# One norm product a head, weight signs on ScalarE, wider value rows and early fills in an attention and expert kernel on one core

## The chip, the cores and the metric

The kernel runs on one core of a Trainium2 chip. The core has TensorE (PE: matrix products; PEld is its loading of the stationary operand), VectorE (DVE), ScalarE (ACT), GpSimd (POOL) and SyncE (SP), which here only starts the transfers. Each engine works through its own list of instructions in order and waits at semaphores. The metric is the time of one execution in microseconds on the device; less is better.

## What is computed

Four batches of 768 tokens with eight heads of 64 go through an attention with a window of 16 to each side and 24 pooled keys and values (a maximum over 32 keys, a mean over 32 values), and the result through a gated layer with 512 features and 1,024 inner ones:

```python
k_sum = k.reshape(B, H, nb, block, D).max(axis=3)
v_sum = v.reshape(B, H, nb, block, D).mean(axis=3)
scores_s = scale * np.einsum('bhsd,bhnd->bhsn', q, k_sum) + np.log(block)
scores_all = np.concatenate([np.where(mask_l, scores_l, -1e9), scores_s], axis=-1)
a = np.exp(scores_all - scores_all.max(-1, keepdims=True))
x = np.matmul(a / (a.sum(-1, keepdims=True) + 1e-09), np.concatenate([v, v_sum], axis=2))
...
xk = mu_k * x + (1.0 - mu_k) * x_prev
xr = mu_r * x + (1.0 - mu_r) * x_prev
k = np.maximum(xk @ w_k, 0.0)
out = 1.0 / (1.0 + np.exp(-(xr @ w_r))) * (k * k @ w_v)
```

The weights are sent as 64-bit floats, in pairs of 32-bit words, and are turned into 32-bit floats on the chip.

## The kernel before

The work is cut into eight stages, one for each half (384 tokens) of each batch. In every stage there are four attention units, one for each pair of heads. A unit (`unit`) computes the scores of 64-query windows against 120 keys each (L466, twelve products of two passes each), adds the mask and takes the maximum on VectorE (L477), the exponential with its sum on ScalarE (L481), the inverse of the sums on VectorE (L487, L488), multiplies by it on GpSimd (`norm`, L493: three instructions of 120 columns for each of the two heads), transposes on TensorE (L500), copies the transposed weights out (L504) and multiplies by v (L513). Then the stage mixes neighbouring tokens (`mix`, L535 to L549), computes the gate (L567 to L569; in the first stage L580, in full float32) with its sigmoid (L558), and runs eight expert steps: a product with a column block of w_k (`first`, L601), ReLU and square (L608, L610), and a product with a row block of w_v (`second`, L627). The first stage works in float32 with unsplit weights. From the second on each weight and each activation is split into two parts (`split`, L349 to L352) and three products replace one.

Weights come in through `weight`: a load into one of three `st` buffers (L310), a product of the high words with 2^-112 on ScalarE or GpSimd (L318, L321), a shift of the low words into the single buffer `we` (L325), the sign taken from the high words and put into `we` (L328), and a join of both into the weight (L332), the last three on VectorE. `load_set` brings in k and v of a pair (L367, L371); v has 120 rows: 48 keys to each side of 24 rows for the pooled values, which are spread into it (L431, L440). GpSimd's list also holds a reload instruction, shown as ISA, which the framework puts ahead of the first instruction that needs it.

Nothing is issued in the order of the source. `Plan` takes every operation with its reads and writes, its due time and its length from the table `LENGTH`, and `schedule` lays them out engine by engine: of the operations that are ready it takes the one that can start first, then the one due first. The order that comes out is fixed and is what each engine's list holds. A transfer is counted with `DMA_NS_PER_BYTE`, and operations named in `LOCKS` are held apart from GpSimd's. Fills (`warm`, L680) are products of the identity with itself whose result nobody reads; they take a buffer of the `mm` pool and are dropped when the first gate product is placed:

```python
if o.name == "gate32" and spare:
    for w in spare:
        ...
    ready["PE"] = [x for x in ready["PE"] if x[0].name != "warm"]
```

Of the kernel before, what the change touches and what calls it, by code (L numbers as in the profile page):

```python
# [20 lines left out]
P = 128  # L21
# [21 lines left out]
    result=695, wbits=340, wor=612, wsub=612, tiny=60,  # L43
    exp=380, pts=380, vm=160, mixa=520, cast=405, relu=525, square=530, sigmoid=500, wscale=570, wcast=530,
    norm=345, wscale_p=640, wcast_p=640, mixa_p=860, kcopy_p=630, evac_a=375, fill=735,
)
TAIL = dict(PE=0, DVE=85, ACT=95, POOL=0, SP=0)
LATENCY = dict(PE=260, DVE=110, ACT=110, POOL=150, SP=0)
DMA_NS_PER_BYTE = 1 / 290.0
DMA_FIXED = 2000  # L50
# [6 lines left out]
SLACK = 400  # L57
WARM = 150
COLD = 10000
EARLY = 15000  # L60
# [38 lines left out]
class Plan:  # L99
# [36 lines left out]
    def schedule(self):  # L136
# [24 lines left out]
        for o in self.ops:  # L161
            if not waiting[o]:
                released(o)
        spare = [o for o in self.ops if o.name == "warm"]
        while any(ready.values()):
            best = None
            for e, now in engines.items():
                pick = None
                for o, at in ready[e]:
                    start, need, ok = max(at, now, o.due - EARLY if e == "SP" else 0), {}, True  # L170
# [49 lines left out]
            order.append(o)  # L220
            if o.name == "gate32" and spare:

                for w in spare:
                    for x in w.bufs:
                        x.left -= 1
                        if not x.left:
                            free_slots[x.pool].append((start, x.place))
                spare = []
                ready["PE"] = [x for x in ready["PE"] if x[0].name != "warm"]
            if o.name == "warm":  # L230
                spare.remove(o)
            for s in o.succ:
# [7 lines left out]
def tile_kernel(ctx: ExitStack, tc: tile.TileContext, q, k, vT, v, mask, ident, pool, sel, mu, w_k, w_v, w_r, out):  # L240
# [60 lines left out]
    def weight(name, i, src, last, due=None):  # L301
        st, we, wc = buf("st"), buf("we"), buf("wc")
        wf = w_f[name, i] = buf("wc") if last else buf("w", F32, False)
        shape = src.shape
        whole = [(wc, 0)]

        def load():
            s = src.bitcast(U32)
            d = st.t.rearrange("p (c a) -> p c a", c=shape[1]) if len(shape) == 3 else st.t
            nc.sync.dma_start(out=d, in_=s)  # L310

        def words():
            w = st.t.rearrange("p (a b) -> p a b", b=2)
            return w[:, :, 1], w[:, :, 0]


        def scale_act():
            nc.scalar.activation(wc.t.bitcast(F32), words()[0].bitcast(F32), AF.Copy, scale=2.0**-112)  # L318

        def scale_pool():  # L320
            nc.gpsimd.tensor_scalar(  # L321
                out=wc.t.bitcast(F32), in0=words()[0].bitcast(F32), scalar1=2.0**-112, scalar2=1.0, op0=ALU.mult, op1=ALU.mult)

        def low():
            nc.vector.tensor_scalar(out=we.t, in0=words()[1], scalar1=29, scalar2=None, op0=ALU.logical_shift_right)  # L325

        def sign():
            nc.vector.scalar_tensor_tensor(  # L328
                out=we.t, in0=words()[0], scalar=0x80000000, in1=we.t, op0=ALU.bitwise_and, op1=ALU.bitwise_or)

        def join():
            nc.vector.scalar_tensor_tensor(  # L332
                out=wf.t.bitcast(U32), in0=wc.t, scalar=3, in1=we.t, op0=ALU.logical_shift_left, op1=ALU.bitwise_or)

        op("SP", "load", due, load, writes=[(st, 0)], size=P * 4096)
        op("ACT", "wscale", None, scale_act, reads=[(st, 0)], writes=whole, other=("POOL", "wscale_p", scale_pool))
        op("DVE", "wbits", None, low, reads=[(st, 0)], writes=[(we, 0)])
        op("DVE", "wor", None, sign, reads=[(st, 0), (we, 0)], writes=[(we, 0)])
        op("DVE", "wor", None, join, reads=[(we, 0), *whole], writes=[(wf, 0)])

# [20 lines left out]
    def load_set(b, p):  # L361
# [83 lines left out]
    def unit(b, p, hf, e, due):  # L445
# [45 lines left out]
        for h in range(2):  # L491
            for i in range(NSL):
                op("POOL", "norm", None, lambda h=h, i=i: nc.gpsimd.tensor_scalar(  # L493
                    out=y[h].t[:, i, :], in0=y[h].t[:, i, :], scalar1=rc.t[:, NSL * h + i:NSL * h + i + 1],
                    scalar2=1.0, op0=ALU.mult, op1=ALU.mult),
                   reads=[(y[h], i), (rc, 0)], writes=[(y[h], i)])

# [77 lines left out]
    def gate_parts(x, z):  # L575

        ps = [buf("mm") for _ in range(NTT)]
        for p in range(NPAIR):
            for t in range(NTT):
                op("PE", "gate32", GATE0 - (NPAIR - 1 - p) * FIRST + 930 * t, lambda p=p, t=t: nc.tensor.matmul(  # L580
                    ps[t].t, x[p].t[:, t * P:(t + 1) * P], w_f["wr", p].t, start=(p == 0), stop=(p == NPAIR - 1)),
                   reads=[(x[p], 0), (w_f["wr", p], 0), *([(ps[t], 0)] if p else [])], writes=[(ps[t], 0)])
# [89 lines left out]
    for i in range(NCK):  # L672
        weight("wr", i, w_r[i * P:(i + 1) * P, :], False)
# [4 lines left out]
    spare = buf("mm", F32, False)  # L678
    for _ in range(WARM):
        op("PE", "warm", 1.0e8, lambda: nc.tensor.matmul(  # L680
            spare.t[:, 0:P], ident_sb, ident_sb, start=True, stop=True), reads=IDENT, writes=[(spare, 0)])
    sets, gates = [], []
# [120 lines left out]
```

## Time and profile before

| | us |
|---|---|
| median of 3 runs (lowest, highest) | 474.1 (472.27, 476.43) |
| the profiled execution | 475.29 |
| its span, first to last instruction | 473.5 |

The granted TensorE clock is 0.993 on the mean. The page's picture of the span in 40 slices of 11.8 us shows each engine's busy share and the clock in tenths:

```profile
PE   2798799989899999999999999999999999999996
DVE  3599789989453566527554565529354554222223
ACT  3578987878785756418886756428886655231311
POOL 0453470734133201302442201304242201000000
PEclk9999889999999999999999999999999999999999
DMA  7995368986110209807200219707100010001001
```

The first ten slices hold the loading of all weights, the first stage and most of the preparation of the second; from then on the stages repeat. Rows of a timeline give start, length, engine, line, operation, output and inputs, shape and count, and in brackets the idle time before and what ended it. Rows of groups give the busy time, the mean of one instruction in ns, and the idle time before.

### The profile page before, as it was taken

What the parts mean: (1) busy time and instruction counts of PE and PEld (TensorE: products, weight loads), DVE (VectorE), ACT (ScalarE), POOL (GpSimd) and SP (SyncE); (2) the same over time, 40 slices, a digit from 0 to 9 for tenths busy, and PEclk for the clock granted to TensorE, in tenths of its full rate; (3) what the DMA queues carried; (4) which work ended last, traced back from release to release, by engine and by line L of the source; (5) the groups of instructions that cost most, each with busy time, mean ns of one, the idle gap of its engine ahead of it and who ended that gap; (6) DMA issues with size and microseconds to landing.
All of it is one profiled execution on the core that took longest, in us unless ns stands there. A gap on an engine that the chain in (4) does not pass through costs nothing.

```text
span 473.5 us, 9475 instructions
## 1 busy us (share of the span) xinstructions
PE 447.6 (95%) x3438; PEld 357.9 (76%) x3438; DVE 267.0 (56%) x865; ACT 292.6 (62%) x815; POOL 112.5 (24%) x236
## 2 busy tenths in 40 slices
PE   2798799989899999999999999999999999999996
PEld 2664455546688888997778888997778889888995
DVE  3599789989453566527554565529354554222223
ACT  3578987878785756418886756428886655231311
POOL 0453470734133201302442201304242201000000
PEclk9999889999999999999999999999999999999999
DMA  7995368986110209807200219707100010001001
GB/s 245 257 261 158 105 207 262 289 263 148 51 59 12 68 1 304 211 0 228 60 8 9 78 37 301 212 1 219 35 9 9 12 43 26 1 0 68 0 1 66
DMA packets 27013, 51.16 MB, mean 108 GB/s; under 512 B 2903, under 2 KB 14807, under 8 KB 26967
## 3 DMA queue, kind: packets, MB, share of 16 engines
q1 hardware_dynamic: 26967, 50.56, 36.7%
q8 instruction: 27, 0.44, 0.4%
q14 instruction: 19, 0.16, 0.1%
HBM read 42.49 MB, written 6.29 MB: 103 GB/s over the span
## 4 chain that ended last, share of the span: by engine, by line
PE 67%; ACT 12%; DVE 8%; DMA 8%; issue 2%; POOL 1%; SPq 1%; ACTq 0%; POOLq 0%; DVEq 0%
PE mm L627 23%; PE mm L601 22%; ACT y L481 5%; PE pt L500 4%; PE av L513 4%; DMA kt<-in_k 3%; PE mm L567 3%; PE mm L569 3%; PE mm L568 3%; PE sc L466 2%; DMA pool_sb<-in_pool 2%; PE mm L580 2%; ACT L481 2%; DMA st<-in_w_k 1%; POOL y L493 1%
## 5 line engine op out<-in xcount | busy, mean ns | idle before, releaser
L601 PE MATMUL mm<-xs,w 128*128 128x384 f32 x736 | 152.1, 355 | 0.6 <-DVE w L332 0.6
L601 PEld LDWEIGHTS mm<-xs,w 128*128 128x128 f32 x736 | 131.3, 190 | 13.9 <-issue 3.7
L493 POOL TENSOR_SCALAR y<-y,rc 128x120 f32<-128x120 f32 x192 | 93.9, 507 | 156.1 <-DVE rc L488 131.6
L627 PE MATMUL mm<-w,kh 128*128 128x512 f32 x336 | 91.9, 402 | 0.0
L608 ACT ACTIVATE r<-mm 128x384 f32<-128x384 f32 x64 | 31.2, 488 | 93.9 <-PE mm L601 93.8
L481 ACT ACTIVATE y<-y,mn 128x120 f32<-128x120 f32 x192 | 73.5, 386 | 10.7 <-DVE mn L477 10.4
L627 PEld LDWEIGHTS mm<-w,kh 128*128 128x128 f32 x336 | 60.7, 188 | 11.1 <-DVE kl L616 0.2
L614 DVE CAST kh<-r 128x384 fp32r<-128x384 f32 x44 | 15.9, 362 | 74.9 <-ACT r L610 74.8
L477 DVE CUSTOM_DVE_ANT_0 y<-sc,mask_sb 128x120 f32<-128x120 f32 x192 | 42.5, 277 | 22.9 <-PE sc L466 19.6
L627 PE MATMUL mm<-w,kl 128*128 128x512 f32 x168 | 52.4, 407 | 0.1
L549 DVE TENSOR_TENSOR xs<-xa,xs 128x384 fp32r<-128x384 f32 x56 | 30.4, 558 | 23.6 <-ACT xs L547 23.2
L500 PE MATMUL pt<-ident_sb,y 128*120 128x128 f32 x192 | 33.9, 285 | 6.4 <-POOL y L493 6.0
L504 ACT COPY pts<-pt 120x384 f32<-120x384 f32 x64 | 30.3, 473 | 15.6 <-PE pt L500 15.4
L466 PE MATMUL sc<-kt,qt 64*64 64x120 f32 x768 | 30.4, 289 | 8.6 <-DMA pool_sb<-in_pool 6.8
L500 PEld LDWEIGHTS pt<-ident_sb,y 128*120 128x120 f32 x192 | 22.8, 139 | 19.0 <-POOL y L493 9.6
L481 ACT ACTIVATION_READ_ACCUMULATOR y<-y,mn 128x1 f32 x192 | 36.3, 189 | 0.0
L541 DVE SCALAR_TENSOR_TENSOR xa<-vx,mu_sb,xa 128x384 f32<-128x384 f32 x56 | 33.8, 630 | 2.7 <-ACT xa L535 1.8
L627 PEld LDWEIGHTS mm<-w,kl 128*128 128x128 f32 x168 | 30.0, 188 | 6.5 <-DVE kl L616 0.5
L466 PEld LDWEIGHTS sc<-kt,qt 64*64 64x64 f32 x768 | 22.2, 143 | 16.7 <-DVE kt L393 6.8
L567 PE MATMUL mm<-w,xs 128*128 128x512 f32 x84 | 33.6, 400 | 1.1 <-ACT r L608 0.8
L610 ACT ACTIVATE r<-r 128x384 f32<-128x384 f32 x64 | 33.6, 525 | 1.2
L616 DVE TENSOR_TENSOR kl<-r,kh 128x384 fp32r<-128x384 f32 x56 | 31.7, 566 | 4.3 <-ACT kh L615 1.3
(64 smaller groups left out, 548.1 us busy)
## 6 DMA issues: line engine op xcount, KB each, us to landing
vx<-in_v SPq DMA_DIRECT2D x32, 360.0 KB
kt<-in_k SPq DMA_DIRECT2D x15, 544.0 KB
qt<-in_q SPq DMA_DIRECT2D x32, 192.0 KB
out<-z SPq DMA_DIRECT2D x24, 256.0 KB
st<-in_vT SPq DMA_DIRECT2D x12, 384.0 KB
st<-in_w_k SPq DMA_DIRECT2D x8, 512.0 KB
st<-in_w_v SPq DMA_DIRECT2D x8, 512.0 KB
st<-in_w_r SPq DMA_DIRECT2D x4, 512.0 KB
```

Of the source, the lines that this page charges most:

```text
L466: nc.tensor.matmul(sc[h].t[cs, i, 0:NK], qt.t[hs, n * QW:(n + 1) * QW], kt.t[hs, w * KB:w * KB + NK], start=True, stop=True,)
L477: op("DVE", "mask", None, lambda h=h, i=i, var=var: nc.vector.tensor_tensor_reduce(out=y[h].t[:, i, :], in0=sc[h].t[:, i, 0:NK], in1=mask_ ...
L481: op("ACT", "exp", None, lambda h=h, i=i: nc.scalar.activation(y[h].t[:, i, :], y[h].t[:, i, :], AF.Exp, bias=mn[h].t[:, i:i + 1], scale=-1.0,
L493: op("POOL", "norm", None, lambda h=h, i=i: nc.gpsimd.tensor_scalar(out=y[h].t[:, i, :], in0=y[h].t[:, i, :], scalar1=rc.t[:, NSL * h + i: ...
L500: nc.tensor.transpose(out=pt[h].t[0:NK, i * P:(i + 1) * P], in_=y[h].t[:, i, :], identity=ident_sb)
L541: op("DVE", "mixd", None, lambda: nc.vector.scalar_tensor_tensor(out=xa.t, in0=xt.t[:, 1 + lo:1 + lo + HT], scalar=mu_sb[:, which, p:p + 1 ...
L567: nc.tensor.matmul(ps.t, xh.t[:, ts], h, start=(p == 0), stop=False)
L601: nc.tensor.matmul(ps.t[:, 0:HT], w.t[:, p * P:(p + 1) * P], (x[p] if single else x[p][s]).t, start=(n == 0), stop=(n == len(terms) * NPAI ...
L608: op("ACT", "relu", None, lambda: nc.scalar.activation(r.t, ps.t[:, 0:HT], AF.Relu), reads=[(ps, 0)], writes=[(r, 0)])
L610: op("ACT", "square", None, lambda: nc.scalar.activation(r.t, r.t, AF.Square), reads=[(r, 0)], writes=[(r, 0)])
L616: op("DVE", "sub", None, lambda: nc.vector.tensor_tensor(out=kl.t, in0=r.t, in1=kh.t.bitcast(F32), op=ALU.subtract), reads=[(r, 0), (kh, 0 ...
L627: nc.tensor.matmul(acc[t].t, a.t[:, t * P:(t + 1) * P], v.bitcast(F32) if single else v, start=start, stop=stop)
```

## The change

There are six parts.

1. **Norms.** The three `norm` instructions of a head become one product of the whole 128 x 360 block with the inverse sums, each repeated over 120 columns. The table's `norm` goes from 345 to 750.
2. **Signs.** The scale of the high words becomes a parametric ReLU on ScalarE with slope -2^32 for negative words, which puts the sign where the join's shift moves it to the top. The sign instruction on VectorE goes, and so does GpSimd as the other engine for the scale.
3. **Values.** v is sent with 128 rows (eight of zeros) in place of 120 and its load writes the whole tile.
4. **Weights.** The blocks of w_k, w_v and w_r are laid out on the host, so that every load is 128 contiguous rows of 4,096 bytes; w_k's were four pieces of 1,024.
5. **Fills.** They multiply a tile of zeros, which GpSimd sets at the start, so that they need no transfer, and write an unused part of the `pt` bank. Up to 260 may be placed; the planner puts one on TensorE wherever nothing else could start within 300 ns, until 110 us of its own count.
6. **First gate.** Its three sigmoids are one operation behind all three gate products. The table's cost of a byte goes from 1/290 to 1/330 ns.

```diff
-            for i in range(NSL):
-                op("POOL", "norm", None, lambda h=h, i=i: nc.gpsimd.tensor_scalar(
-                    out=y[h].t[:, i, :], in0=y[h].t[:, i, :], scalar1=rc.t[:, NSL * h + i:NSL * h + i + 1],
-                    scalar2=1.0, op0=ALU.mult, op1=ALU.mult),
-                   reads=[(y[h], i), (rc, 0)], writes=[(y[h], i)])
+            op("POOL", "norm", None, lambda h=h: nc.gpsimd.tensor_tensor(
+                out=y[h].t, in0=y[h].t, in1=rc.t[:, NSL * h:NSL * h + NSL].unsqueeze(2).broadcast_to([P, NSL, NK]), op=ALU.mult),
+               reads=[(rc, 0)] + [(y[h], i) for i in range(NSL)], writes=[(y[h], i) for i in range(NSL)])
...
-            nc.scalar.activation(wc.t.bitcast(F32), words()[0].bitcast(F32), AF.Copy, scale=2.0**-112)
+            wc.t.bitcast(F32), words(1).bitcast(F32), AF.Prelu, scale=2.0**-112, alpha=-2.0**32),
...
-        def sign():
-            nc.vector.scalar_tensor_tensor(
-                out=we.t, in0=words()[0], scalar=0x80000000, in1=we.t, op0=ALU.bitwise_and, op1=ALU.bitwise_or)
...
-                out=windows(vw[hf]), in_=v[b, p, hf]),
-               writes=[(vw[hf], "a"), (vw[hf], "b")], size=NK * HW * 512)
+                out=vw[hf].t[:, 0:S], in_=v[b, p, hf]),
+               writes=[(vw[hf], "a"), (vw[hf], "b")], size=P * HW * 512)
...
-        weight("wk", j, w_k[:, j * P:(j + 1) * P].rearrange("(c p) n -> p c n", p=P), False)
-        weight("wv", j, w_v[j * P:(j + 1) * P, :], j == NCV - 1)
+        weight("wk", j, w_k[j], False)
+        weight("wv", j, w_v[j], j == NCV - 1)
...
+                if fill and (pick is None or pick[2] > fill[0] + GAP):
+                    pick = None, fill[1], fill[0]
...
+    op("POOL", "tiny", -1.0e6, lambda: nc.gpsimd.memset(zero_sb, 0.0), writes=ZERO)
+    spare = pools["pt"][0][:, 512 - P:512]
     for _ in range(WARM):
-        op("PE", "warm", 1.0e8, lambda: nc.tensor.matmul(
-            spare.t[:, 0:P], ident_sb, ident_sb, start=True, stop=True), reads=IDENT, writes=[(spare, 0)])
+        op("PE", "warm", 1.0e8, lambda: nc.tensor.matmul(spare, zero_sb, zero_sb, start=True, stop=True), reads=ZERO)
...
-        for t in range(NTT):
-            sigmoid(ps[t], z[t])
+        def sigmoids():
+            for t in range(NTT):
+                nc.scalar.activation(z[t].t, ps[t].t, AF.Sigmoid)
+
+        op("ACT", "sigmoid3", None, sigmoids, reads=[(a, 0) for a in ps], writes=[(a, 0) for a in z])
```

The planner lays everything out anew, so the change moves instructions on every engine. Line numbers are those of each kernel. ScalarE around the first gate, before: `z` is the sigmoid's output, `y` a head's scores, `wc` a scaled weight, `r` an expert block.

```order
L558 ACT_TABLE_LOAD
L558 ACTIVATE z_108<-mm_135 128x512
L481 ACT_TABLE_LOAD
L481 ACTIVATE y_91,sm_100<-y_91,mn_95 128x120 x3
L481 ACTIVATE y_92,sm_100<-y_92,mn_96 128x120 x3
L558 ACT_TABLE_LOAD
L558 ACTIVATE z_109<-mm_133 128x512
L558 ACTIVATE z_110<-mm_134 128x512
L318 ACTIVATE wc_127<-st_123 128x512
L608 ACTIVATE r_116<-mm_132 128x384
L610 ACTIVATE r_116<-r_116 128x384
L481 ACT_TABLE_LOAD
```

The same place on ScalarE in the changed kernel:

```order
L456 ACTIVATE y_91,sm_100<-y_91,mn_95 128x120 x3
L456 ACTIVATE y_92,sm_100<-y_92,mn_96 128x120 x3
L559 ACT_TABLE_LOAD
L559 ACTIVATE z_108<-mm_133 128x512
L559 ACTIVATE z_109<-mm_135 128x512
L559 ACTIVATE z_110<-mm_132 128x512
L585 ACTIVATE r_116<-mm_134 128x384
L477 COPY pts_107<-pt_130 120x384
L587 ACTIVATE r_116<-r_116 128x384
L307 ACTIVATE wc_127<-st_123 128x512
L307 ACTIVATE wc_126<-st_124 128x512
L456 ACT_TABLE_LOAD
```

The six exponentials of the unit moved ahead of the sigmoids, and two of the four table loads are gone. Over the whole list there are 20 table loads against 22, and none stands at the parametric ReLU (L307).

VectorE ahead of the last gate product, before (`we`, `wc`, `w`: the weight's parts; `xs`: mixed tokens; `vx`: v):

```order
L325 TENSOR_SCALAR we_125<-st_122 128x512
L352 TENSOR_TENSOR w_0_516<-w_0_495,w_0_500 128x512
L328 SCALAR_TENSOR_TENSOR we_125<-st_122,we_125 128x512
L332 SCALAR_TENSOR_TENSOR w_0_524<-wc_127,we_125 128x512
L325 TENSOR_SCALAR we_125<-st_123 128x512
L328 SCALAR_TENSOR_TENSOR we_125<-st_123,we_125 128x512
L352 TENSOR_TENSOR w_0_559<-w_0_524,w_0_529 128x512
L332 SCALAR_TENSOR_TENSOR w_0_563<-wc_126,we_125 128x512
L541 SCALAR_TENSOR_TENSOR xs_0_561<-vx_79,mu_sb,xs_0_561 128x384
```

And in the changed kernel:

```order
L327 TENSOR_TENSOR w_0_516<-w_0_496,w_0_505 128x512
L514 SCALAR_TENSOR_TENSOR xs_0_513<-vx_76,mu_sb,xs_0_513 128x384
L406 COPY vx_77<-vm_88 24x768
L310 TENSOR_SCALAR we_125<-st_123 128x512
L327 TENSOR_TENSOR w_0_533<-w_0_510,w_0_525 128x512
L312 SCALAR_TENSOR_TENSOR w_0_547<-wc_126,we_125 128x512
L327 TENSOR_TENSOR w_0_555<-w_0_547,w_0_549 128x512
L514 SCALAR_TENSOR_TENSOR xs_0_557<-vx_79,mu_sb,xs_0_557 128x384
```

The sign instructions (L328) are gone from between the shift and the join; one split more stands ahead of the mix of the last pair.

GpSimd's list at the start, before:

```order
L522 MEMSET vx_79 128x1
L493 ISA
L493 TENSOR_SCALAR y_91<-y_91,rc_102 128x120 x3
L493 TENSOR_SCALAR y_92<-y_92,rc_102 128x120 x3
L493 TENSOR_SCALAR y_93<-y_93,rc_103 128x120 x3
L493 TENSOR_SCALAR y_94<-y_94,rc_103 128x120 x3
L431 COPY vx_69<-vm_85 24x768
L321 TENSOR_SCALAR wc_126<-st_122 128x512
```

And in the changed kernel:

```order
L495 MEMSET vx_79 128x1
L368 COPY kt_62<-ks_83 128x12x24
L467 ISA
L467 TENSOR_TENSOR y_91<-y_91,rc_102 128x360
L467 TENSOR_TENSOR y_92<-y_92,rc_102 128x360
L467 TENSOR_TENSOR y_93<-y_93,rc_103 128x360
L406 COPY vx_68<-vm_85 24x768
L467 TENSOR_TENSOR y_94<-y_94,rc_103 128x360
```

The reload (ISA) moved behind a copy of the pooled keys into `kt`, which VectorE made before, and the copy waits for the second pair's keys. TensorE's list begins with 13 fills, has 11 between the first two sets of scores, 7 ahead of the first pooled values, eight more before the gates, and five on either side of the first transposes behind the gates: 49 fills against 15.

More of the change, by code (lines that the diff above doesn't have):

```diff
@@ L43 @@
     result=695, wbits=340, wor=612, wsub=612, tiny=60,
-    exp=380, pts=380, vm=160, mixa=520, cast=405, relu=525, square=530, sigmoid=500, wscale=570, wcast=530,
-    norm=345, wscale_p=640, wcast_p=640, mixa_p=860, kcopy_p=630, evac_a=375, fill=735,
+    exp=380, pts=380, vm=160, mixa=520, cast=405, relu=525, square=530, sigmoid=500, sigmoid3=4000, wscale=570, wcast=530,
+    norm=750, wscale_p=640, wcast_p=640, mixa_p=860, kcopy_p=630, evac_a=375, fill=735,
 )
@@ L48 @@
 LATENCY = dict(PE=260, DVE=110, ACT=110, POOL=150, SP=0)
-DMA_NS_PER_BYTE = 1 / 290.0
+DMA_NS_PER_BYTE = 1 / 330.0
 DMA_FIXED = 2000
@@ L57 @@
 SLACK = 400
-WARM = 150
-COLD = 10000
+WARM = 260
+WARM_END = 110000
+GAP = 300
+COLD = 5000
 EARLY = 15000
@@ L163, in schedule @@
                 released(o)
-        spare = [o for o in self.ops if o.name == "warm"]
         while any(ready.values()):
@@ L167, in schedule @@
             for e, now in engines.items():
-                pick = None
+                pick = fill = None
+                if e == "PE" and now > WARM_END:
+                    ready[e] = [x for x in ready[e] if x[0].name != "warm"]
                 for o, at in ready[e]:
+                    if o.name == "warm":
+                        fill = max(now, at), o
+                        continue
                     start, need, ok = max(at, now, o.due - EARLY if e == "SP" else 0), {}, True
@@ L220, in schedule @@
             order.append(o)
[L221 to L231, printed above, removed]
             for s in o.succ:
@@ L276, in tile_kernel @@
     sel_sb = const.tile([P, NS], F32, name="sel_sb")
-    MASK, IDENT, MU, OM, POOLM, SEL = [((x, 0),) for x in ("mask", "ident", "mu", "om", "pool", "sel")]
+    zero_sb = const.tile([P, P], F32, name="zero_sb")
+    MASK, IDENT, MU, OM, POOLM, SEL, ZERO = [((x, 0),) for x in ("mask", "ident", "mu", "om", "pool", "sel", "zero")]
     op("SP", "load", None, lambda: nc.sync.dma_start(out=mask_sb, in_=mask), writes=MASK, size=P * 3 * NK * 4)
@@ L303, in weight @@
         wf = w_f[name, i] = buf("wc") if last else buf("w", F32, False)
[L304 to L325, printed above, removed]
-        def sign():
-            nc.vector.scalar_tensor_tensor(
-                out=we.t, in0=words()[0], scalar=0x80000000, in1=we.t, op0=ALU.bitwise_and, op1=ALU.bitwise_or)
@@ L331, in join @@
[L331 to L338, printed above, removed]
@@ L339, in weight, with words @@
-        op("DVE", "wor", None, join, reads=[(we, 0), *whole], writes=[(wf, 0)])
+        def words(n):
+            return st.t.rearrange("p (a b) -> p a b", b=2)[:, :, n]
+        op("SP", "load", due, lambda: nc.sync.dma_start(out=st.t, in_=src.bitcast(U32)), writes=[(st, 0)], size=P * 4096)
+        op("ACT", "wscale", None, lambda: nc.scalar.activation(
+            wc.t.bitcast(F32), words(1).bitcast(F32), AF.Prelu, scale=2.0**-112, alpha=-2.0**32),
+           reads=[(st, 0)], writes=[(wc, 0)])
@@ L341, in split @@
+        op("DVE", "wbits", None, lambda: nc.vector.tensor_scalar(
+            out=we.t, in0=words(0), scalar1=29, scalar2=None, op0=ALU.logical_shift_right), reads=[(st, 0)], writes=[(we, 0)])
+        op("DVE", "wor", None, lambda: nc.vector.scalar_tensor_tensor(
+            out=wf.t.bitcast(U32), in0=wc.t, scalar=3, in1=we.t, op0=ALU.logical_shift_left, op1=ALU.bitwise_or),
+           reads=[(we, 0), (wc, 0)], writes=[(wf, 0)])
     def split(name, i):
@@ L787 @@
         "mu": mu.reshape(2, NPAIR, P).transpose(2, 0, 1),
-        "w_k": words(inputs["moe_w_k"]),
-        "w_v": words(inputs["moe_w_v"]),
-        "w_r": words(inputs["moe_w_r"]),
+        "w_k": words(np.asarray(inputs["moe_w_k"]).reshape(NCK, P, NCV, P).transpose(2, 1, 0, 3), NCV),
+        "w_v": words(np.asarray(inputs["moe_w_v"]), NCV),
+        "w_r": words(np.asarray(inputs["moe_w_r"]), NCK),
     }
```

11 lines of the change are left out of this document (5 added, 6 removed).

## Prediction

> **What bounds the kernel now.** I read the totals of the page first, then the busy time by stretch, then TensorE's own waits.
>
> ```profile
> PE 447.6 (95%) x3438; PEld 357.9 (76%) x3438; DVE 267.0 (56%) x865; ACT 292.6 (62%) x815; POOL 112.5 (24%) x236
> ```
>
> TensorE is busy for 95% of the span, so only three things can be won: its idle time, time in which it runs at a lower clock, and work it need not do. The stretches say where those lie (columns: PE, PEld, DVE, ACT, POOL busy, then granted clock, DMA share, GB/s).
>
> ```profile
> 0.00:6.85 6.85, 0.00 (x1) 0.03 (x1) 1.68 (x5) 1.28 (x1) 0.40 (x8) 1.00 0.62 195
> 6.85:20.85 14.00, 9.78 (x111) 7.21 (x112) 7.98 (x45) 7.32 (x34) 5.31 (x13) 1.00 1.04 282
> 20.85:47.60 26.75, 25.28 (x290) 15.61 (x290) 24.18 (x69) 19.99 (x53) 11.46 (x16) 1.00 0.75 210
> 47.60:62.40 14.80, 11.36 (x71) 6.58 (x70) 9.64 (x40) 14.67 (x43) 5.71 (x9) 0.77 0.40 121
> 62.40:130.00 67.60, 62.76 (x489) 38.37 (x489) 57.79 (x180) 53.42 (x147) 28.17 (x51) 1.00 0.70 205
> 130.00:469.80 339.80, 338.37 (x2490) 290.06 (x2486) 165.09 (x533) 195.88 (x542) 61.45 (x140) 1.00 0.24 70
> 55.00:61.80 6.80, 6.79 (x34) 4.10 (x34) 3.83 (x20) 6.74 (x23) 2.50 (x6) 0.50 0.55 157
> ```
>
> From 130 us on TensorE idles 1.43 us of 339.8: nothing is to be had there. Before it, TensorE waits for others: VectorE is 90% busy from 20.85 to 47.6 (24.18 of 26.75), ScalarE 99% from 47.6 to 62.4, and in that stretch TensorE falls to half clock for 6.8 us. So the first 130 us decide, by when the gate products end (47.6) and when the first product with w_v starts (62.4).
>
> TensorE's rows there, and ScalarE's table loads between them (start, length, what):
>
> ```profile
> 44.77 2.84 PE L580 MATMUL mm<-w,xs 128*128 128x512 f32 x6 [1.47 <-DVE xs L541]
> 47.45 2.74 PE L601 MATMUL mm<-xs,w 128*128 128x384 f32 x8
> 50.12 0.84 PE L466 MATMUL sc<-kt,qt 64*64 64x120 f32 x24
> 53.95 0.33 PE L500 MATMUL pt<-ident_sb,y 128*120 128x128 f32 x1 [2.98 <-POOL y L493]
> 54.72 0.81 PE L500 MATMUL pt<-ident_sb,y 128*120 128x128 f32 x2 [0.44 <-POOL y L493]
> 55.45 1.71 PE L466 MATMUL sc<-kt,qt 64*64 64x120 f32 x24
> 57.10 5.17 PE L601 MATMUL mm<-xs,w 128*128 128x384 f32 x8
> 62.10 0.49 PE L500 MATMUL pt<-ident_sb,y 128*120 128x128 f32 x3
> 46.83 1.28 ACT L558 ACT_TABLE_LOAD   x1
> 48.74 1.28 ACT L481 ACT_TABLE_LOAD   x1
> 52.43 1.28 ACT L558 ACT_TABLE_LOAD   x1
> 56.33 1.28 ACT L481 ACT_TABLE_LOAD   x1
> ```
>
> The wait of 2.98 us is named after GpSimd, but its product waited for the exponentials, and these for two table switches; then the same 24 score products take 1.71 instead of 0.84 us and the eight expert products 5.17 instead of 2.74, both in the half-clock stretch.
>
> **The change, part by part.** The profiled execution took 475.29 us (span 473.5 and 1.8 around it); the median of the runs is 474.1, so 1.2 us come off at the end.
>
> ```profile
> L328 DVE SCALAR_TENSOR_TENSOR we<-st,we 128x512 uint32<-128x512 uint32 x20 | 14.8, 738 | 0.1
> L328 DVE SCALAR_TENSOR_TENSOR we<-st,we 128x512 uint32<-128x512 uint32 x5 | 3.9, 773 | 0.0
> SPq L310 <- DVE we L328: 51.9, 17, 6.2
> L318 ACT ACTIVATE wc<-st 128x512 f32<-128x512 f32 x15 | 10.2, 678 | 2.9 <-DMA st<-in_w_k 2.1 <-DMA st<-in_w_v 0.7
> L535 ACT ACTIVATE xa<-vx,om_sb 128x384 f32<-128x384 f32 x46 | 26.8, 611 | 3.1 <-DVE xs L549 2.4 <-DVE vx L524 0.5
> L547 ACT CAST xs<-xa 128x384 fp32r<-128x384 f32 x56 | 27.7, 506 | 2.1 <-DVE xa L541 2.1
> ```
>
> *Signs.* VectorE loses 20 instructions, 14.8 us, all before 130 us; five of them, 3.9 us, stand between 20.85 and 47.6, where it is full, so I take -3.9 for the end of the gates. The weight loads on SP waited 51.9 us in 17 waits for just this instruction; they start earlier too. ScalarE scales all 20 weights now, five more: 5 x 0.678 = +3.4. Its other function may cost nothing more, or one more operand: at most 611 - 506 = 105 ns, 2.1 us over 20; I take nothing, since the order has no table load at these instructions. Against that its order sheds 5 weight casts, 6 first mix products, 3 other casts (14 at 0.5 to 0.6 us) and 2 table loads of 1.28, and takes 6 evictions from VectorE at about 0.5: some -7.5, so ScalarE is relieved by about 4 us over the span.
>
> ```profile
> 17.45 2.06 POOL L493 TENSOR_SCALAR y<-y,rc 128x120 f32<-128x120 f32 x6 [2.20 <-DVE rc L488]
> 33.80 5.40 POOL L493 TENSOR_SCALAR y<-y,rc 128x120 f32<-128x120 f32 x6 [0.42 <-DVE rc L488]
> L493 POOL TENSOR_SCALAR y<-y,rc 128x120 f32<-128x120 f32 x192 | 93.9, 507 | 156.1 <-DVE rc L488 131.6
> L321 POOL TENSOR_SCALAR wc<-st 128x512 f32<-128x512 f32 x5 | 3.8, 764 | 21.6 <-DMA qt<-in_q 7.4 <-DVE kg L385 6.2 <-DMA st<-in_w_r 5.5
> PE pt L500 <- POOL y L493: 6.0, 5, 3.0
> ```
>
> *Norms.* Undisturbed, three instructions take 1.03 us (2.06 for six), on the mean 3 x 507 = 1.52, under a full VectorE 2.70 (5.40 for six). One product of 360 columns with two inputs isn't in the trace. Below: one input of 360 columns, between 343 ns (120) and 764 (512), is 0.60. Above: the three as they are, 1.52. I take 1.0: one start and one possible wait for VectorE in place of three. [...] Heads come sooner by 0.5 us, but TensorE waited only 6.0 us for them in all, and 3.0 of these are counted below. The last pair of the first half (the row with 5.40) stands ahead of its gate product: -1 there, between 0 and -3.4.
>
> *v rows and weight rows.* Eight v loads fall in the first 30 us.
>
> ```profile
> 22.00:23.50 1.50, 1.50 (x30) 1.31 (x29) 0.97 (x4) 0.70 (x3) 0.00 (x0) 1.00 0.97 227
> 69.00:71.00 2.00, 2.00 (x6) 0.90 (x5) 1.97 (x4) 2.00 (x5) 1.73 (x3) 1.00 1.01 346
> 14.63 1.51 PE L405 MATMUL mm<-vx,pool_sb 120*32 120x128 f32 x24 [2.44 <-DMA pool_sb<-in_pool]
> 13.02 2.22 POOL L493 TENSOR_SCALAR y<-y,rc 128x120 f32<-128x120 f32 x6 [12.09 <-DVE ks L389]
> ```
>
> While v comes in, all engines are busy (0.97) and move 227 GB/s; beside weight loads, 346. Eight loads of 360 KB, 2.95 MB, take 13.0 us at the one rate; 3.15 MB at the other 9.1. Bounds for the DMA queue: from -3.9 to +0.9 (6.7% more bytes at the old rate). TensorE's wait at 14.63 lies behind the first two of them and would end about 1 us sooner. What takes that back: GpSimd's order has its one reload instruction (ISA) moved behind the first copy into kt, so it starts near 10 us instead of 1. Its length is hidden before 13.02 in the 12.09 us of idle: anything from 0 to 12. I set the two against each other, 0, with -1.9 and +4 as ends. The w_k loads are most of the stretch with 346 GB/s already, so their longer rows count nothing. On SP the first 38 loads keep their order; after them one w_k load passes a q and a kt load, and a vT load a v load, too little to price.
>
> *The gates' sigmoids and the fills.* Four table loads around the gates become two: -2.6 on an engine that is 99% busy there. In the order the first exponentials of the second half now stand ahead of the sigmoids, so the 2.98 us wait and, with ten fill products in the remaining gaps, the half clock should go. Between the gates and the first w_v product TensorE then has: 2.74 + 0.84 + 0.33 + 2.74 + 0.33 = 7.0 us of work and ten fills.
>
> ```profile
> 19.32 1.93 PEld L680 LDWEIGHTS mm<-ident_sb 128*128 128x128 f32 x10
> 24.32 0.61 PE L680 MATMUL mm<-ident_sb 128*128 128x128 f32 x4
> ```
>
> A fill is two passes: five took 1.93 us at the low clock (0.39 each), two 0.61 at the full one (0.3 at most): ten cost 2 to 3. That makes 9 to 10 where 14.8 stood: -5 at best; the two table loads alone are -2.6. I take -4.5, nearer to TensorE's own count since its named wait has gone. The other 39 fills (49 in all against 15) stand mostly before 20 us, where TensorE is idle 4.2 of 14 us and idle altogether before 6.85; the eleven between the first two sets of scores can hold the second set up by 2 us if the clock is still low, hidden by the DMA wait at 14.63.
>
> *After that.* From 62.4 to 130 TensorE idles 4.84 us. Half of it is weights, table loads and norms; but everything comes 9 us earlier and finds less ready. I take -2, between -4.8 and +5.
>
> Sum: -3.9 - 1 + 0 - 4.5 - 2 = -11.4, so 475.3 becomes 463.9 profiled and 462.7, say 463, as a median.
>
> **Rivals.**
> *ScalarE takes over as the bound.* It is 99% busy from 47.6 to 62.4 and 79% after; with the same work between 47.6 and 130 in 7 us less it stands near 88%. Then only signs and table loads count and 4 us of new waits come: 470.
> [...]
> *The fills don't hold the clock.* Zero operands may not count as activity. Then the stretch at 55 stays at half clock: (5.17 - 2.74) + (1.71 - 0.84) = 3.3 more, 466.
> *Slower: the product on GpSimd.* Before, the planner's table had 0.345 an instruction, 1.04 a head, against 1.52 in the trace, and some 54 heads from 62.4 on cost TensorE few waits (6.0 us in all, 0.11 a head): 0.37 of lateness was absorbed. Now the table has 0.75. At T a head TensorE would wait T - 0.75 - 0.37, 54 times. That eats the 11.4 at T = 1.33, and from 1.42 on the kernel is more than 1% slower. At 1.5, what three took: 54 x 0.38 = 20.5, so 483. For it: 2.70 a head under a full VectorE. Against it: one product waits once, not three times, and VectorE loses work just there.
>
> **Chances.** Forecast 0.60 (own range 456 to 468); ScalarE 0.14; the DMA term 0.09; clock 0.08; GpSimd 0.09. A measurement of this kernel tells about 1% from no change. Faster by over 1% (below 469.4): 0.60 + 0.09 + 0.08 = 0.77; within 1%: 0.14; slower: 0.09. Low end: -3.9 - 3.4 - 1.9 up to the gates, -5 behind them and -4.8 after make 455; high end 471 takes in ScalarE's case and leaves GpSimd's and a tail out.
>
> **What would show it.** VectorE with 20 fewer instructions and the gate products ending near 43; two table loads between them and the first w_v product, 9 to 10 us apart; no half clock after 20 us; one norm a head at 0.8 to 1.2 us; v stretches above 300 GB/s. Wrong: a ScalarE row in front of TensorE's waits between 50 and 130, TensorE's wait for GpSimd above 10 us, or the first norm later than 16 us.

## The result and the profile after

| | before | changed |
|---|---|---|
| median of 11 executions, us (lowest, highest) | 474.22 (472.27, 476.43) | 470.95 (465.86, 471.38) |
| the profiled execution, us; its span | 475.29; 473.5 | 471.38; 469.6 |
| mean granted TensorE clock in it | 0.993 | 0.988 |

The ratio is 0.9914, with a 95% interval of 0.9886 to 0.9942: 3.3 us less, where 11 had been forecast. The page of the changed kernel begins so:

```profile
PE 454.0 (97%) x3506; PEld 366.0 (78%) x3506; DVE 263.8 (56%) x842; ACT 286.9 (61%) x810; POOL 78.5 (17%) x115
PE   8989999988999999999899999999989999999996
ACT  3887889876775657167966459247966555231321
PEclk9999999999999999999999999999989999999999
```

VectorE is only 3 us less busy, though 14.8 us of sign instructions are gone. TensorE's row now has digits below 9 in the middle of the span, at the 20th and 30th slice, where it had none before. The busy time by stretch, cut where the gate products end (42.46) and where the first w_v product starts (51.32):

```profile
6.85:20.85 14.00, 13.43 (x218) 11.22 (x221) 10.15 (x56) 9.79 (x44) 4.35 (x6) 1.00 1.02 382
20.85:42.46 21.61, 20.20 (x211) 10.98 (x204) 19.54 (x52) 17.13 (x45) 7.27 (x8) 1.00 0.54 197
42.46:51.32 8.86, 8.86 (x67) 6.25 (x67) 7.59 (x28) 7.81 (x20) 4.13 (x5) 1.00 0.47 150
51.32:130.00 78.68, 74.73 (x604) 47.91 (x603) 60.09 (x194) 64.13 (x191) 20.42 (x28) 0.98 0.57 193
130.00:465.00 335.00, 331.26 (x2393) 284.78 (x2392) 163.51 (x510) 186.75 (x513) 41.81 (x60) 0.99 0.21 70
```

The early part went as forecast or better. The loads run at 382 GB/s in the second stretch, where it was 282, the gate products end 5.1 us earlier (42.46 against 47.6), and the way from there to the first w_v product is 8.86 us against 14.80, at full clock. But from 130 us on TensorE idles 3.74 us where it idled 1.43, and the clock column falls below 1.00 in the last two rows. Followed through the starts of TensorE's products in the two timelines, the lead is won and lost here:

| TensorE, us | before | changed | lead |
|---|---|---|---|
| stage 1: first w_v product | 62.43 | 51.32 | 11.1 |
| stage 2: first gate product | 109.34 | 97.14 | 12.2 |
| stage 3: first gate product | 171.94 | 162.81 | 9.1 |
| stage 4: first gate product | 220.35 | 211.34 | 9.0 |
| stage 5: first gate product | 277.75 | 271.19 | 6.6 |
| stage 6: first gate product | 326.51 | 319.82 | 6.7 |
| stage 7: first gate product | 383.89 | 379.67 | 4.2 |
| end of the span | 473.5 | 469.6 | 3.9 |

So 8 us of 12.2 are given back, in three places: the gates of stage 2, and the first expert steps of stages 4 and 6. The first three rows of TensorE's waits in the changed kernel (us in all, times, longest):

```profile
PE av L486 <- ACT pts L477: 3.6, 2, 1.8
PE pt L473 <- ACT vm L412: 1.7, 1, 1.7
PE mm L540 <- ACT z L531: 1.7, 1, 1.7
```

And TensorE's timeline at the second place (start, length; in brackets the idle time ahead):

```profile
229.22 0.52 PE L473 MATMUL pt<-ident_sb,y 128*120 128x128 f32 x3
229.49 1.64 PE L604 MATMUL mm<-w,kh 128*128 128x512 f32 x6
231.06 0.33 PE L486 MATMUL av<-pts,vx 120*64 120x64 f32 x2
233.18 1.53 PE L486 MATMUL av<-pts,vx 120*64 120x64 f32 x22 [1.79 <-ACT pts L477]
234.64 0.39 PE L395 MATMUL pt<-ident_sb,vs 128*24 128x128 f32 x1
234.96 1.48 PE L441 MATMUL sc<-kt,qt 64*64 64x120 f32 x24
```

The transposes end at 229.73. The value products need their copy into `pts`, and wait for it for 1.79 us. Then 24 score products, which take 0.85 us elsewhere, take 1.48. ScalarE's rows say what the copy stood behind:

```profile
228.62 0.46 ACT L477 COPY pts<-pt 120x384 f32<-120x384 f32 x1
229.09 1.28 ACT L456 ACT_TABLE_LOAD   x1
230.39 0.40 ACT L456 ACTIVATE y<-y,mn 128x120 f32<-128x120 f32 x1
...
232.30 0.38 ACT L456 ACTIVATE y<-y,mn 128x120 f32<-128x120 f32 x1
232.58 0.19 ACT L456 ACTIVATION_READ_ACCUMULATOR y<-y,mn 128x1 f32 x1
232.67 0.46 ACT L477 COPY pts<-pt 120x384 f32<-120x384 f32 x1
```

The copy of the second head (232.67) is issued behind a table load of 1.28 us and six exponentials. The planner's order puts it there, and the planner's table has no entry for a table load, so in its count ScalarE is through with the exponentials 1.28 us sooner. What follows the wait is shown by stretches of 3.41 us, cut where the granted clock changes (columns: length, PE, PEld, DVE, ACT, POOL, clock):

```profile
113.77:117.19 3.42, 1.72 (x12) 1.61 (x12) 1.33 (x3) 2.16 (x5) 1.42 (x3) 1.00 0.05 10
117.19:120.60 3.41, 3.41 (x45) 2.29 (x46) 1.13 (x11) 2.30 (x5) 0.00 (x0) 1.00 0.41 115
...
229.83:233.24 3.41, 1.61 (x10) 0.98 (x9) 1.06 (x5) 3.40 (x15) 0.00 (x0) 1.00 0.00 0
233.24:236.65 3.41, 3.41 (x49) 2.76 (x50) 1.71 (x3) 1.74 (x5) 1.53 (x2) 0.50 0.00 0
```

The whole wait lies in the stretch from 229.83, so TensorE is busy for 1.61 of its 3.41 us, and the next stretch runs at half clock, just as long. It is the same at 103.53 and at 342.47. The wait at 114 us (1.70; before the change one of 1.68 stood at 123) leaves 1.72 busy, and no half clock follows it. The eleven executions of the changed kernel differ by this: six with a mean clock of 0.988 or 0.989 took 470.95 to 471.38, four with 0.992 or 0.993 took 469.29 to 469.76, and one with 0.998 took 465.86.

My theory, **A**: the early gain is real; it is given back by three waits that the new order opens where ScalarE is later than planned (1.67 + 1.79 + 1.79 us), and by the half clock behind each (up to 1.7 us each). The rival, **B**: the waits alone do it, and the half clock falls where TensorE has slack. Others followed from the parts of the forecast that the profile doesn't show one by one.

### The profile page after: what moved, and what is told of

Read it like the earlier page. It is cut to its first block, busy times and chain, and to the rows that moved or that the text cites. A ratio compares the mean times of both kernels' runs of the same rounds, so it can differ in the third digit from the quotient of the medians.

```text
span 469.6 us, 9507 instructions
## 1 busy us (share of the span) xinstructions
PE 454.0 (97%) x3506; PEld 366.0 (78%) x3506; DVE 263.8 (56%) x842; ACT 286.9 (61%) x810; POOL 78.5 (17%) x115
## 4 chain that ended last, share of the span: by engine, by line
PE 77%; ACT 11%; DVE 7%; issue 2%; DMA 1%; SPq 0%; DVEq 0%; ACTq 0%
PE mm L604 26%; PE mm L578 25%; PE av L486 4%; PE sc L441 4%; ACT y L456 4%; PE pt L473 4%; PE mm L540 3%; PE mm L541 3%; PE mm L542 3%; PE pt L658 2%; ACT L456 1%; PE mm L553 1%; DVE w L312 1%; ACT pts L477 1%; ACT L531 1%
## 5 line engine op out<-in xcount | busy, mean ns | idle before, releaser
L578 PE MATMUL mm<-xs,w 128*128 128x384 f32 x736 | 149.7, 352 | 0.2 <-ACT r L585 0.2
L467 POOL TENSOR_TENSOR y<-y,rc 128x360 f32<-128x360 f32 x64 | 53.8, 861 | 198.3 <-DVE rc L463 145.7
L456 ACT ACTIVATE y<-y,mn 128x120 f32<-128x120 f32 x192 | 73.5, 385 | 11.4 <-DVE mn L452 11.1
L604 PEld LDWEIGHTS mm<-w,kh 128*128 128x128 f32 x336 | 60.8, 188 | 11.1 <-issue 0.5
L591 DVE CAST kh<-r 128x384 fp32r<-128x384 f32 x47 | 20.5, 436 | 78.0 <-ACT r L587 77.9
L486 PEld LDWEIGHTS av<-pts,vx 120*64 120x64 f32 x768 | 26.1, 140 | 16.2 <-issue 11.0
L593 DVE TENSOR_TENSOR kl<-r,kh 128x384 fp32r<-128x384 f32 x56 | 33.1, 591 | 7.1 <-ACT kh L592 4.1
L486 PE MATMUL av<-pts,vx 120*64 120x64 f32 x768 | 30.8, 229 | 3.6 <-ACT pts L477 3.6
```

The lines of the kernel that those rows point to most:

```text
L456: op("ACT", "exp", None, lambda h=h, i=i: nc.scalar.activation(y[h].t[:, i, :], y[h].t[:, i, :], AF.Exp, bias=mn[h].t[:, i:i + 1], scale=-1.0,
L467: op("POOL", "norm", None, lambda h=h: nc.gpsimd.tensor_tensor(out=y[h].t, in0=y[h].t, in1=rc.t[:, NSL * h:NSL * h + NSL].unsqueeze(2).bro ...
L486: nc.tensor.matmul(av.t[hs, w * QW:(w + 1) * QW], windows(vw)[:, w, hs], pts[h].t[:, i, c * QW:(c + 1) * QW], start=True, stop=True,)
L578: nc.tensor.matmul(ps.t[:, 0:HT], w.t[:, p * P:(p + 1) * P], (x[p] if single else x[p][s]).t, start=(n == 0), stop=(n == len(terms) * NPAI ...
L593: op("DVE", "sub", None, lambda: nc.vector.tensor_tensor(out=kl.t, in0=r.t, in1=kh.t.bitcast(F32), op=ALU.subtract), reads=[(r, 0), (kh, 0 ...
L604: nc.tensor.matmul(acc[t].t, a.t[:, t * P:(t + 1) * P], v.bitcast(F32) if single else v, start=start, stop=stop)
```

## The experiments

The order of the changed kernel is kept, so that one thing differs, unless the text says otherwise. Times are medians; the ratio is to the kernel before on the same chip, with its 95% interval. The changed kernel stands at 470.95 and 0.9914.

### The waits and the half clock

**Fills in the waits.** Ahead of four products, by their number in the plan:

```diff
+    gaps = {956: 6, 811: 6, 1258: 7, 1700: 7}
     for o in order:
+        for _ in range(gaps.get(o.n, 0)):
+            nc.tensor.matmul(spare, zero_sb, zero_sb, start=True, stop=True)
         o.emit()
```

> The changed kernel with zero products put into four waits of TensorE: six each ahead of the second gate product of stage 2 (idle 1.67 us) and ahead of the transposes at 115.6 (1.70), seven each ahead of the two value products at 231 and 340 us (1.79 each). Nothing else moves. Theory A (the lead won before 100 us is given back by half-clock stretches of 3.41 us that follow these waits, 1.7 us each, besides the waits themselves): no half clock after 100 us, 471 - 3 x 1.7 = 466 us, and less spread between executions. Theory B (the lead is given back by the waits alone, the half clock falls where TensorE would wait anyway): 470 to 472. Fills that come late and hold the next products up: above 472.

472.62 us (0.9959, 0.9933 to 0.9986): slower, and the experiment did not do what it was made for. TensorE's waits in it say why:

```profile
PE pt L691 <- ACT pts L477: 4.1, 2, 2.0
```

The fills write into the bank of the transposes, and so waited for the very copy that TensorE was waiting for; then they stood ahead of the value products. The six meant for the wait at 114 us missed it: that wait stays at 1.69, and they run at 119, ahead of the next transposes, where TensorE did not wait. The half clock went at 103 and at 231 us and stayed at 340.

**Real work in the waits.** Three products of the next step that were long ready are moved ahead of the waiting value products, at 231 and 340 us:

```diff
+    at = {o.n: o for o in order}
+    for low, values in ((1429, 1258), (1871, 1700)):
+        order.remove(at[low])
+        order.insert(order.index(at[values]), at[low])
```

> The changed kernel with, at 231 and 340 us, the three products with the low part of the activations (0.87 us of real work, which stand behind the waiting value products) put ahead of them. Theory A: each wait falls from 1.79 to 0.92 us and no half clock follows there; the one at 103.5 stays: 471 - 2 x (0.87 + 1.7) = 465.9 us. Theory B: only 2 x 0.87 are won, 469.2 us. If ScalarE sets the pace of that place whatever TensorE does meanwhile (the next transposes wait instead): 470 to 471.

465.38 us (0.9810, 0.9773 to 0.9847), as theory A had it, with a clock of 1.00. The wait is 1.09 us now:

```profile
228.87 0.86 PE L604 MATMUL mm<-w,kl 128*128 128x512 f32 x3
229.66 0.33 PE L486 MATMUL av<-pts,vx 120*64 120x64 f32 x2
231.08 0.91 PE L486 MATMUL av<-pts,vx 120*64 120x64 f32 x22 [1.09 <-ACT pts L477]
```

Stages 4 and 6 take 57.7 us from gate to gate instead of 59.85. The wait of 1.67 at 103 is still there, but in this execution it is split between two stretches (0.65 and 1.03 idle), and no half clock followed: part of the gain here is that. Later runs build on this one as the second run.

**Both.** The fills are those of the first run, three in place of seven at 231 and 340 us.

> The moved products of the run before and fills in what is left of all four waits (six, six, three, three). Theory A: 471 - 1.74 - 5.1 = 464.1 us with a granted clock of 0.998, close to the fastest of the eleven executions of the changed kernel (465.86 at 0.998). Theory B: 469.

468.36 us (0.9866, 0.9822 to 0.9911). The clock stayed up (0.999), but the fills again stood behind the copy and ahead of the work, and at 119 us where there is no wait. Against the run before they cost 3 us: 1.4 between the gates of stages 2 and 3, and 0.8 in each of stages 4 and 6.

**Fills that can start.** The fills at 231 and 340 us write unused columns of the `av` bank:

```diff
+    gaps = {956: (6, spare), 811: (6, spare), 1258: (7, spare_av), 1700: (7, spare_av)}
```

> As the first run with fills, but the seven fills at 231 and at 340 us write unused columns of the av bank, so that they no longer have to wait for the copy of the transposes (in the first run they waited for it and came behind the wait). The waits themselves stay. Theory A (idle time of more than half of a 3.41 us stretch brings half clock in the next one): no half clock after 100 us, 466 us, spread under 2 us. Theory B (waits alone): 470 to 471.

467.96 us (0.9867, 0.9838 to 0.9897), five executions within 0.5 us. At the place where the changed kernel fell to half clock:

```profile
229.75:233.16 3.41, 3.18 (x36) 2.78 (x36) 0.62 (x3) 3.40 (x16) 0.31 (x1) 1.00 0.00 0
233.16:236.58 3.42, 3.42 (x51) 2.93 (x46) 2.72 (x13) 2.55 (x10) 1.22 (x2) 1.00 0.14 26
```

The value products still come as late, yet stages 4 and 6 take 58.3 and 58.4 us against 59.85: a half-clock stretch costs 1.5 us, and the stage-2 gates are 1.5 us shorter too. Theory B falls. The total is 2 us above what A expected. Of this, 1.4 lie between stages 2 and 3 (65.53 us from gate to gate, 64.07 in the second run), where six fills stand at 119 us and not in the wait at 114:

```profile
113.68 0.52 PE L475 MATMUL pt<-ident_sb,y 128*120 128x128 f32 x3 [1.69 <-ACT vm L414]
119.25 1.60 PE L694 MATMUL pt<-zero_sb 128*128 128x128 f32 x12
```

### Where the waits come from

**One number of the table.**

```diff
-    norm=750, wscale_p=640, ...
+    norm=1035, wscale_p=640, ...
```

> The changed kernel with one number of the planner's table changed back: a head's norm counts 1035 (three times the 345 of before) in place of 750; the instructions are the same, their order is not: the copies of the transposes stand ahead of the six exponentials again at 231 and 340 us. If the new price made the waits: no wait of over 1 us and no half clock there, 466 us (465 if the wait at 103 goes too). If other parts of the change made them: 470 to 471.

468.45 us (0.9892, 0.9856 to 0.9929). The waits of 1.79 us are gone, so the new price of the norms did make them; stage 4 takes 57.9 us. But stage 6 takes 59.8, since shorter waits add up to 1.72 us in one stretch and half clock follows, and the wait at the gates of stage 2 has grown, with 6.8 us of half clock behind it (its profiled execution, at 471.85, is 3.4 above its median):

```profile
PE mm L540 <- ACT z L531: 4.5, 1, 4.5
```

So this price only decides where the lateness falls.

**Table loads in the planner.** Every change between exponential and sigmoid now counts 1.28 us:

```diff
+LOAD = 1280
+TABLES = dict(exp=0, sigmoid=1, sigmoid3=1)
...
             o.cost, o.emit = o.ways[e]
+            if e == "ACT" and o.name in TABLES and TABLES[o.name] != table:
+                table = TABLES[o.name]
+                o.cost += LOAD
```

> The changed kernel with a planner that counts 1280 for every change between exponential and sigmoid on ScalarE, which it took for nothing. If the lead was lost because ScalarE ran late by these loads against the plan: the waits at 103, 231 and 340 us (5.2 us) and the half clock behind them (5.1) go, 460 to 462 us. If ScalarE is the bound there in any order and the waits only move: 465 to 466.

458.49 us (0.9668, 0.9639 to 0.9697), better than A expected. Three rows are all that is left of TensorE's waits:

```profile
PE pt L664 <- ACT pts L483: 1.8, 3, 0.6
PE pt L664 <- POOL zero_sb L661: 1.0, 1, 1.0
PE mm L559 <- DVE xs L520: 0.3, 1, 0.3
```

ScalarE's timeline at the second place has the copy behind one exponential:

```profile
223.29 1.28 ACT L462 ACT_TABLE_LOAD   x1
224.58 0.40 ACT L462 ACTIVATE y<-y,mn 128x120 f32<-128x120 f32 x1
224.88 0.19 ACT L462 ACTIVATION_READ_ACCUMULATOR y<-y,mn 128x1 f32 x1
224.98 0.46 ACT L483 COPY pts<-pt 120x384 f32<-120x384 f32 x1
```

There are 20 table loads in both; only the order differs. ScalarE was not the bound. And the gain goes further than the waits that had come with the change. Stage 4, first in the kernel before and then here:

```profile
220.35:277.75 57.40, 56.75 (x530) 47.68 (x528) 28.28 (x114) 43.31 (x130) 17.91 (x43) 1.00 0.19 58
206.24:262.10 55.86, 55.86 (x529) 47.40 (x526) 29.72 (x115) 40.44 (x124) 13.33 (x19) 1.00 0.21 65
```

Stage 6 does the same (57.38 and 55.88), so 3.0 us were to be had in these two stages, more than half of them from time that counts as busy before.

**The same planner on the kernel before.**

> The kernel before, with only the planner's 1280 for each change of ScalarE's table added. If the change is worth the 11 us of the prediction and only the order hid it, this kernel stays 11 us or more behind the changed one with the same planner (458.5): 469.5 or later, so little faster than 474. If most of what the price of table loads won has nothing to do with the change: 463 or earlier, as much as it won on the changed kernel (12.5).

469.48 us (0.9894, 0.9854 to 0.9934). With table loads priced on both sides, the change takes the time from 469.5 to 458.5: 11.0 us, or 10.7 by the two ratios, which fit better as the runs were made on two chips. The price alone wins about 5 us on the kernel before, against 12.5 on the changed one. Two plans are compared here, each with luck of its own: the new one of before ends its gate products at 50.19 us, 2.6 later than its old one, and has half-clock stretches at 45.4 and 69.3 us, and its executions spread from 466.9 to 471.4.

### The parts

**No fills.** They are taken out of the finished order:

```diff
-    order = plan.schedule()
+    order = [o for o in plan.schedule() if o.name != "warm"]
```

> The changed kernel with its order kept and all 49 fills taken out of TensorE's list. If the fills hold the clock, as the prediction had it: half clock until about 20 us as in the kernel before and again around 50 us, the gate products end 2 to 4 us later than 42.5, the first w_v product starts 3 to 6 later than 51.3, and the time is 474 to 477. If zero products have no part in it: the same 42.5 and 51.3 within 1 us, 470 to 471.

467.56 us (0.9853, 0.9802 to 0.9904). TensorE's clock opens at 16.3 us, not at 4.55, and the gate products end at 43.21; but the first w_v product starts at 50.5, for the ten fills ahead of it had cost 1.6 us, and no half clock comes there without them. The time lies below both expectations. In the order with priced table loads:

> The order of the run before, with all fills left out. From the run without fills (gate products 0.75 us later, first w_v product 0.8 earlier): within 1 us of the run before. If the fills are worth what the clock gains before 20 us: 2 to 4 us slower.

455.88 us (0.9615, 0.9583 to 0.9648), the fastest so far; its executions (455.4 to 456.5) and those with fills (458.0 to 458.9) don't overlap. The fills cost 2.6 us.

**Four of the other five parts** were put back one by one into the kernel of the second run (465.38 us, gate products to 41.96, first w_v product at 50.81), since its profile has no half clock to blur them. The rows of the weights and the price of a byte were not tried alone.

```diff
+                for i in range(NSL):
+                    nc.gpsimd.tensor_scalar(out=y[h].t[:, i, :], ...)
```

> The kernel of the second run (465.4 us, gate products to 41.96, first w_v product at 50.81) with its order kept and each head's one norm product taken apart into the three instructions of before. If the product is worth the 1 us that the prediction gave it, ahead of the gates alone: gate products end 0 to 2 later, 465.5 to 467.5. If every head's later end counts, 64 x (1.52 - 0.86) = 42 us at most: above 475.

463.77 us (0.9771, 0.9750 to 0.9793): not slower, if anything faster. In the order with priced table loads and no fills:

> The order of the run with priced table loads and no fills (455.9), kept, with each head's one norm product taken apart into the three instructions of before. If the one product slows VectorE also in this order (VectorE 11 us busier in all, and 1.6 us of time in the second run's order): 454 to 455. If VectorE has the room now that TensorE never waits there: 455.5 to 456.5.

455.87 us (0.9617, 0.9582 to 0.9653), against 455.88. The product is worth nothing in time. In the changed kernel it is

```profile
L467 POOL TENSOR_TENSOR y<-y,rc 128x360 f32<-128x360 f32 x64 | 53.8, 861 | 198.3 <-DVE rc L463 145.7
```

In the second run's order it takes GpSimd's busy time from 114.4 to 79.2 us, but VectorE pays: its casts into `kh` take 421 ns in the second run,

```profile
L591 DVE CAST kh<-r 128x384 fp32r<-128x384 f32 x47 | 19.8, 421 | 77.3 <-ACT r L587 77.2
```

and 364 with three norms:

```profile
L596 DVE CAST kh<-r 128x384 fp32r<-128x384 f32 x47 | 17.1, 364 | 79.1 <-ACT r L592 79.1
```

```diff
-            wc.t.bitcast(F32), words(1).bitcast(F32), AF.Prelu, scale=2.0**-112, alpha=-2.0**32),
+            wc.t.bitcast(F32), words(1).bitcast(F32), AF.Copy, scale=2.0**-112),
...
+            nc.vector.scalar_tensor_tensor(
+                out=we.t, in0=words(1), scalar=0x80000000, in1=we.t, op0=ALU.bitwise_and, op1=ALU.bitwise_or)
```

> The kernel of the second run with its order kept; the scale on ScalarE is a plain copy with 2^-112 again, and the sign instruction stands again on VectorE behind each of the 20 shifts (14.8 us). If five of them stood in a full VectorE ahead of the gates, as the prediction had it: gate products end 3 to 5 us later than 41.96, first w_v product 3 to 6 later than 50.81, 469 to 471. If VectorE had the room: 465 to 466.

475.70 us (1.0028, 1.0015 to 1.0040): putting the signs back costs 10.3 us, more than the whole change measured, in an order that was planned without them. The gate products end 2.6 us later and the first w_v product starts 3.5 later, but the gates of stage 2 start 11.1 later. VectorE stays behind all through the first stage, and the largest of TensorE's new waits, at 96 us, is for it. A half-clock stretch follows that wait (from 100.1 us) and makes up 1.4 of the 10.3:

```profile
PE pt L399 <- DVE vs L396: 3.5, 1, 3.5
```

```diff
-                out=vw[hf].t[:, 0:S], in_=v[b, p, hf]),
+                out=vw[hf].t[0:NK, 0:S], in_=v[b, p, hf, 0:NK]),
```

> The kernel of the second run with the v loads cut to the 120 rows that are read; order and all else the same. If 128 rows are what makes the early transfers faster: the stretch from 6.85 to 20.85 us falls from 380 GB/s to about 280, the first pooled-values product comes 1 to 2 us later than 13, the gate products end 1 to 3 later, 466 to 468. [...]

469.47 us (0.9884, 0.9854 to 0.9915). The stretch from 6.85 us in the second run:

```profile
6.85:20.85 14.00, 13.43 (x231) 11.24 (x224) 10.18 (x56) 10.28 (x45) 4.72 (x7) 1.00 1.04 395
```

and with 120 rows:

```profile
6.85:20.85 14.00, 12.12 (x185) 9.95 (x179) 9.25 (x52) 9.01 (x41) 4.35 (x6) 1.00 1.03 300
```

The DMA engines are busy throughout in both (mean shares 1.04 and 1.03), and 95 GB/s are missing. Gate products and first w_v product both come 2.2 us later.

```diff
+                if t == 0:
+                    nc.scalar.activation(spare_sb, mu_sb[:, 0, 0:1], AF.Exp)
```

> The kernel of the second run with one exponential of one column put between the first and second sigmoid of the first gate, whose result nobody reads: ScalarE changes its table twice more there (2 x 1.28 and 0.2), as before the change. If these loads were on the path, as the prediction's -2.6 has it: the first w_v product starts 2 to 3 us later than 50.81, 467 to 468.5. If ScalarE had room behind the gates: 465 to 466.

466.76 us (0.9839, 0.9814 to 0.9864). The first w_v product starts at 50.73, no later than without them, but what comes right behind it waits for ScalarE's copy and then for its ReLU:

```profile
54.74 0.91 PE L487 MATMUL av<-pts,vx 120*64 120x64 f32 x22 [0.94 <-ACT pts L478]
56.27 2.85 PE L581 MATMUL mm<-xs,w 128*128 128x384 f32 x8 [0.61 <-ACT r L588]
```

In the second run these expert products start at 54.63, so TensorE is 1.6 us later. ScalarE has room for about 1 us of the two loads: in the second run it waits 1.01 us ahead of its copy at 48.10. The rest is on the path, one step behind the place where it was looked for. The 1.4 us in the time fit this, but the two intervals overlap.

## Why the prediction was off, step by step

- **The step that failed** is "From 130 us on TensorE idles 1.43 us of 339.8: nothing is to be had there", by which those stages got no term in the sum. The change plans them anew, and a TensorE that is busy for 99% has no slack to take a new wait: 4.9 us were lost there, in stages 4 and 6, by waits for ScalarE and the half clock behind them. Nor is it true of a gain: with table loads priced, the same two stages take 3.0 us less than before. The step "After that" failed as well: put at -2, it came out at +2.0 (a lead of 11.1 us at the first w_v product, of 9.1 at the gates of stage 3), since 3.1 were lost between 97 and 109 us. Up to the first w_v product -9.4 were forecast and -11.1 came. The measured 3.3 (3.9 between the two profiles) are what is left.
- **The total.** That 11.0 us come out where table loads are priced on both sides, against the forecast 11.4, is mostly luck: the terms don't have the sizes given to them, as the next points show.
- **The half clock.** "No half clock after 20 us" was wrong. I read the stretch at 55 us as a consequence of table loads, and not as what a wait of about 1.8 us can bring: in the changed kernel's profile half clock followed both stretches with 1.79 us of TensorE idle, at 229.83 and at 339.05.
- **Signs, -3.9.** Mis-sized: 10.3 us in the order kept, 1.4 of them by the half clock. I counted the five instructions in the stretch where VectorE is 90% busy; but with all 20 back the delay grows from 2.6 us at the gate products to 11.1 at the gates of stage 2, so the others count too.
- **v rows, set against the late reload as 0.** The rows are worth 2.2 us by 51 us and up to 4 in the medians; what makes the rest is not shown. The first norm transposes came at 13.84 (16.06 before), so nothing shows that the reload took anything back. The chance of 0.09 for the DMA term stood for 128 rows that are no faster than 120. No run shows that: with everything else alike, the stretch from 6.85 us moved 395 GB/s with 128 rows and 300 with 120.
- **Norms, -1.** Nothing, by two experiments. The instruction itself took 0.86 us against the 1.0 I had taken. So GpSimd's rival (from 1.33 on) stayed out. TensorE waited 0.2 us for it in all; that its price in the table moves the order was not thought of.
- **Gates to the first w_v product, -4.5.** 8.86 us came, "9 to 10" was said, and the count of 7.0 without the fills was near (7.3 in the run without them). The table loads, -2.6, hold up not this product but the ones right behind it, by 1.6 us. What was shed is the 2.98 us wait and the half clock of before; which single edit of the order shed them was not tried.
- **ScalarE takes over** (470) came nearest in time, by a wait for ScalarE as it says. But ScalarE was not the bound: the same work in another order takes 458.5, and its load from the gates to 130 us was 82% (71.94 of 87.54), not "near 88%" (which should have been 90 by the numbers there). **The fills don't hold the clock** (466): zero operands do open it (at 4.55 us, 16.3 without them), and it wasn't worth having.

## What to carry to other kernels

A change that lets a planner lay out everything anew must be priced in every stage that it lays out, also where its idle time says that nothing is to be won: here those stages lost 4.9 us in one order and won 3.0 in another. When a large early gain shrinks towards the end, table the start of the same product in both traces stage by stage; the steps in that column name the places. A planner that leaves out a cost of 1.28 us for 20 table loads can put urgent work behind a load that it does not see. One entry for it was worth 12.5 us on the changed kernel, more than the change itself was measured at, and about 5 on the kernel before.

## What the runs showed of the hardware

- The clock changes by stretches of 3.413 us on a grid that lies differently from profile to profile: in the changed kernel's the half-clock stretches start at 103.53, 233.24 and 342.47 us, 38 and 32 times 3.413 apart; in that of before, one of twice the length starts at 54.99, 14.2 times 3.413 ahead of 103.53. Over all profiles, full-clock stretches ahead of the kernel's end with 1.67 and 1.72 us of TensorE idle in them (once each), about 1.79 (four times) and all with 1.97 or more were followed by half clock; nine with 1.60 to 1.69 and one with 1.80 were not, nor any with less. So the same wait of 1.67 us at 103 costs 1.5 more in one execution and nothing in the next.
- Products of zeros open the clock: with them, from 0.99 us on, it opened at 4.55 us of the span (a product took 432 ns between 1 and 4.3 us, 284 from 4.6 on), without them at 16.3, and the first 24 score products take 0.85 us (at 6.73) against 1.48 (at 6.15, and at 6.34 in the run without fills and with three norms).
- The parametric ReLU takes no longer than the copy it replaces (675 against 678 ns), and no table load stands at it.
- One product of 360 columns on GpSimd slows VectorE more than three of 120: VectorE is 263.8 us busy against 252.4 in the second run's order, for the same 842 instructions, and 264.0 against 256.2 in the one with priced table loads.
